# Linear attention with complex gates and an MLP on one core: another order table for all five engines, and the ACT table loads listed up front

## The chip, the cores and the metric

The kernel runs on one core of a Trainium2 chip. A core has a matrix engine (TensorE, PE in the profile), three engines for element-wise work (VectorE is DVE, ScalarE is ACT, GpSimd is POOL) and queues for transfers, of which this kernel uses the one of SyncE (SP). Each engine works through its own list of instructions in the order in which it was written, and waits at the head of its list until what that instruction needs has been made. The metric is the device time of the whole program in microseconds, the median of several runs. The profile is one more execution, recorded by the hardware profiler.

## The reference

```python
# q, k, v, a_re, a_im: (B=4, H=8, S=768, D=48)
mag = sqrt(a_re**2 + a_im**2)
scale = minimum(mag, 0.999) / (mag + 1e-6)
a = scale * (a_re + 1j * a_im)
for t in range(S):                      # S_ is D x D for each batch and head
    S_ = a[:, :, t, :, None] * S_ + k[:, :, t, :, None] * v[:, :, t, None, :]
    y[:, :, t] = einsum('bhd,bhde->bhe', q[:, :, t], S_.real)
x = y.transpose(0, 2, 1, 3).reshape(3072, 384)
h = x @ w_in                            # 384 x 2048
g = h * tanh(log1p(exp(h)))
out = g @ w_out                         # 2048 x 384
```

All tensors are fp32. In the kernel the recurrence over time becomes, for each chunk of 128 tokens, two small matrix products for each head: products of q and k inside the chunk, weighted by the running product of the gates, and a term with the state that the chunk before left.

## The kernel before, in words

The 3072 tokens are worked in 12 units of 256, three units to a batch, each of two chunks of 128. A unit passes through three stages, and while one unit is in the MLP the next ones are in the earlier stages.

The first stage, `ew_steps`, works out the running product of the gates: its size through logarithms and exponentials, its angle through an arctangent, sums along time and sines. ACT does the functions and DVE most of the rest. ACT needs one function table for logarithm and exponential and another for arctangent and sine, and a table load (`ACT_TABLE_LOAD`) stands between stretches of the two kinds. `window` holds the steps of a unit that need the second table. `phi2` (L456) is the step that brings an angle into one turn. The stage ends in `turn1` and `turn2`, which multiply q and k by the product (L497) and send the result through DMAs (`relay`, L493) into the tile `T`, in which heads instead of channels lie on the partitions.

The second stage, `attn_steps`, is made, for each chunk, of these parts: `pkn`, a transpose of k on PE (L569) that ACT copies into the tile `kn` (L570); `pa`, the products of q and k (L613, later units L601), which DVE masks into `am` (L615, L604); `ypsum`, the sum of `am` times v and of q times the old state (L628), which ACT copies to `y` (L633); `pd`, the new part of the state, from `kn` and v (L648), which DVE adds to the state `S` (L653, L655, L656); and DMAs that turn `y` into the rows `xf` of the MLP (L669, L682).

The third stage, `moe_steps`, runs over 8 pairs of 128 columns of the hidden layer: `ph` is the first product (L715; for the first half of the first unit L711, which takes plain fp32 operands), an elementwise chain `e` on ACT and DVE makes g from it (L719 to L725, on ACT recorded as L250), g is split into a coarse and a fine part (`gh`, `gl`, L282 and L283), `po` is the second product (L752, L748), and DVE evicts it as `o` (L767), which a DMA writes out (L768). Three terms (coarse times coarse, fine times coarse, coarse times fine) make a product here, so `ph` and `po` are by far the most work of PE.

The weights arrive as 64-bit integers in which the bits of the given numbers lie, one tile `raw0` to `raw15` for each block (L303). Each is converted by one ACT operation (recorded as L250), two DVE operations (L313, L314) and an addition on POOL (L316), and later split (L282, L283).

`spin` puts 84 filler matmuls (`junk`, L540) into PE's list, on a constant tile; nothing reads their result. 40 of them wait for the first `phi2`, 44 for the copy to `y`.

What sets the order of the work: the program is first written down stage by stage, and then `in_order` chains the instructions of each engine by the table `ORDER`, a text for each of PE, DVE, Activation, Pool and SP. A number is an instruction's place among those of its engine as written, and "+n" stands for n that follow each other. So the engine's list is exactly the table's:

```python
for run in text.split():
    first, _, count = run.partition("+")
    for n in range(int(first), int(first) + int(count or 1)):
        if last is not None:
            tc.add_manual_dep(own[n], last.name, order, reason="order of the engine")
        last = own[n]
```

Of the kernel before, what the change touches and what calls it, by code (L numbers as in the profile page):

```python
# [28 lines left out]
TU = 256  # L29
NU = S // TU  # L30
UNITS = B * NU
# [24 lines left out]
KU = 3  # L56
PU = 3
# [952 lines left out]
```

## Time and profile before

| | us |
|---|---|
| median of 3 runs | 573.38 (571.77 to 573.8) |
| the profiled execution's own time | 573.63 |
| its span in the trace | 571.9 |
| PE busy in the span | 547.7 (96%) |
| DVE busy | 481.1 (84%) |
| ACT busy | 469.4 (82%) |
| POOL busy | 40.5 (7%) |

The span runs from the first recorded work of the program to its last; the run's own time is 1.7 us longer. Busy shares are means over the whole span, and the stages have different limits, so the shares alone don't say what the time hangs on. Matmuls overlap each other in their pipeline, so starts are a better guide than durations when one counts what a matmul costs. A matmul of fp32 operands can show as two records. The mean granted clock of PE over the span is 0.993.

### The profile page before, as it was taken

Reading aid. Unit: us, or ns where it says so; the run is one execution under the profiler, and the core shown is the slowest. Engines: PE = TensorE matmul, PEld = TensorE weight load, DVE = VectorE, ACT = ScalarE, POOL = GpSimd, SP = SyncE. Lnnn points to the kernel's source line nnn. Section 1 sums busy time; section 2 is a strip of 40 time slices with the busy share of each in tenths; the row PEclk is TensorE's granted clock in tenths of the full one; section 3 lists DMA queues with packets and bytes.
Section 4 is the critical chain, followed back from the end, with each engine's and each line's share of the span. In section 5 each row is a group of like instructions: output and inputs, shape, how many; then the busy total and the mean of one; then the engine's idle time right before and its main releaser. Section 6 shows DMA issues by size and latency. Waiting matters only on the chain.

```text
span 571.9 us, 13326 instructions
## 1 busy us (share of the span) xinstructions
PE 547.7 (96%) x5254; PEld 509.9 (89%) x5254; DVE 481.1 (84%) x865; ACT 469.4 (82%) x753; POOL 40.5 (7%) x55
## 2 busy tenths in 40 slices
PE   0889999999999999999999999999999999999996
PEld 0458878789999999999999999999999999999996
DVE  6989999999999998988988999887897887554543
ACT  6898999999987899799898988888978777446662
POOL 2111413330010000000000000000000000000000
PEclk9979999999999999999999999999999999999999
DMA  8778935906553647606547437317426425301000
GB/s 281 241 237 261 329 118 139 278 22 193 162 164 107 188 126 191 170 16 182 142 137 202 132 91 226 115 36 216 139 75 173 116 70 145 105 21 37 1 29 32
DMA packets 69059, 80.69 MB, mean 141 GB/s; under 512 B 6144, under 2 KB 60672, under 8 KB 68992
## 3 DMA queue, kind: packets, MB, share of 16 engines
q1 hardware_dynamic: 68992, 79.80, 47.1%
q8 instruction: 42, 0.69, 0.5%
q14 instruction: 25, 0.20, 0.1%
HBM read 44.63 MB, written 11.40 MB: 98 GB/s over the span
## 4 chain that ended last, share of the span: by engine, by line
PE 93%; DVE 2%; DMA 2%; SPq 1%; ACT 0%; issue 0%; DVEq 0%
PE ph L715 35%; PE po L752 33%; PE ypsum L628 7%; PE pa L601 5%; PE po L748 4%; PE pd L648 3%; PE junk L540 2%; PE ph L711 2%; PE pa L613 2%; DMA raw<-w_in 1%; PE pkn L569 1%; SPq L350 1%; DMA T<-QK 0%; SPq L357 0%; DVE X L497 0%
## 5 line engine op out<-in xcount | busy, mean ns | idle before, releaser
L715 PE MATMUL ph<-xH,w 128*128 128x256 f32 x1104 | 226.1, 287 | 0.0
L752 PE MATMUL po<-w,gh 128*128 128x384 f32 x704 | 202.9, 339 | 0.0
L250 ACT ACTIVATE e<-e 128x512 f32<-128x512 f32 (+1 forms) x300 | 177.2, 609 | 19.8 <-DVE e L720 17.2
L715 PEld LDWEIGHTS ph<-xH,w 128*128 128x128 f32 x1104 | 180.9, 190 | 2.8 <-issue 0.8
L715 PE MATMUL ph<-xL,w 128*128 128x256 f32 x552 | 156.0, 283 | 0.0
L752 PEld LDWEIGHTS po<-w,gh 128*128 128x128 f32 x704 | 129.4, 189 | 2.1 <-issue 1.3
L752 PE MATMUL po<-w,gl 128*128 128x384 f32 x352 | 118.8, 337 | 0.0
L715 PEld LDWEIGHTS ph<-xL,w 128*128 128x128 f32 x552 | 104.8, 190 | 1.4 <-issue 0.8
L250 ACT ACTIVATE e<-ph 128x512 f32<-128x512 f32 (+1 forms) x100 | 57.1, 572 | 42.9 <-PE ph L715 34.7
L725 DVE SCALAR_TENSOR_TENSOR g<-e,ph 128x512 f32<-128x512 f32 (+1 forms) x100 | 65.7, 657 | 20.1 <-ACT e L250 16.5
L752 PEld LDWEIGHTS po<-w,gl 128*128 128x128 f32 x352 | 66.3, 188 | 0.2
L720 DVE TENSOR_SCALAR e<-e 128x512 f32<-128x512 f32 (+1 forms) x100 | 41.2, 412 | 28.3 <-ACT e L250 28.1
L283 DVE TENSOR_TENSOR gl<-g,gh 128x512 fp32r<-128x512 f32 x88 | 59.9, 682 | 2.9 <-ACT gh L282 2.5
L258 ACT ACT_TABLE_LOAD x47 | 60.3, 1283 | 1.6 <-PEq L966 0.8
L250 ACT ACTIVATE X<-X 128x768 f32<-128x768 f32 (+1 forms) x70 | 51.4, 747 | 3.0 <-DVE X L397 1.9
L540 PE MATMUL junk<-cmask 128*128 128x512 bf16 x84 | 24.2, 443 | 15.4 <-DVE I L456 15.4
L628 PE MATMUL ypsum<-am,V 128*48 128x128 f32 x240 | 36.1, 273 | 1.0 <-DVE am L615 1.0
L316 POOL TENSOR_TENSOR raw<-raw 128x768 int32<-128x768 int32 x16 | 28.5, 1782 | 93.9 <-DVE raw L314 47.2
L282 ACT CAST gh<-g 128x512 fp32r<-128x512 f32 x40 | 24.6, 614 | 10.9 <-PE po L752 10.6
L540 PEld LDWEIGHTS <-cmask 128*128 128x128 bf16 x84 | 9.1, 112 | 27.2 <-issue 21.8
L628 PE MATMUL ypsum<-T,S 96*48 96x128 f32 x320 | 32.5, 277 | 0.0
L250 ACT ACTIVATE X<-R 128x768 f32<-128x768 f32 (+1 forms) x40 | 29.6, 757 | 1.0 <-DVE R L433 1.0
(88 smaller groups left out, 757.3 us busy)
## 6 DMA issues: line engine op xcount, KB each, us to landing
T<-X SPq DMA_DIRECT2D x72, 129.0 KB, 2.5
T<-QK SPq DMA_DIRECT2D x72, 129.0 KB, 2.5
raw<-w_in SPq DMA_DIRECT2D x8, 768.0 KB, 7.1
raw<-w_out SPq DMA_DIRECT2D x8, 768.0 KB, 6.6
kd<-vx SPq DMA_DIRECT2D x45, 128.0 KB, 2.8
kn<-kd SPq DMA_DIRECT2D x15, 384.0 KB, 3.1
V<-v SPq DMA_DIRECT2D x12, 384.0 KB, 4.0
out_dram<-o SPq DMA_DIRECT2D x24, 192.0 KB, 2.2
```

The lines of the kernel that those rows point to most:

```text
L250: ins = nc.scalar.activation(out, in_, func, **kw)
L258: ins = nc.scalar.preload_act_table_set(name)
L282: heng(h, src)
L283: leng(out=lo, in0=src, in1=h.bitcast(F32), op=ALU.subtract)
L316: nc.gpsimd.tensor_tensor(hi, hi, lo, ALU.add)
L540: ins = nc.tensor.matmul(junk, cmask, cmask.unsqueeze(1).broadcast_to([P, 4, P]), start=True, stop=True)
L601: nc.tensor.matmul(pa[row:row + C // 2, i, hi * C // 2:], T[:, 1, hi * C // 2:][:, :C // 2], T[:, 0, hi * C // 2:C], start=True, stop=True)
L628: nc.tensor.matmul(py[64 * par:64 * par + D, i, :], lhs, rhs, start=n == 0, stop=first or n == 1)
L715: nc.tensor.matmul(ph[:, a, :], rows_in(parts[j][:, wp], kt, a), st[xp][:, kt, :], start=n == 0, stop=n == 8)
L720: nc.vector.tensor_scalar_min(e, e, math.exp(20.0))
L725: nc.vector.scalar_tensor_tensor(g, e, 2.5, ph, ALU.subtract, ALU.mult)
L752: nc.tensor.matmul(po[t], gp[:, a, tsl], rows_out(parts[NPAIR + j][:, wp], a), start=j in starts and a == 0 and n == 0, stop=j + 1 in ends ...
```

## The change

Three things are edited. The table `ORDER` is replaced by another for all five engines; it was reached from the old one by moving single instructions. The ACT table loads, which were written where the stretch of each kind began (by `with_trig`, with `act` and `act_set` around them), are now written ahead of everything as one list, `SETS`, and the order table puts them into ACT's list; there are 45 of them instead of 47. And `ew_steps` gets a branch for units from `PIPE` on; as `PIPE` is 99 and there are 12 units, it is never taken.

```diff
+PIPE = 99
...
 ORDER = {
     "PE": """
-        0+24 40+4 48+16 24+4 44+4 28+8 64+16 124+12 36+4 80+16 188+6 96+4 136+4 226+3 248+3 100+4 251+3 229+3 156+16
...
+        0+10 48 40 49 44+2 52+4 50+2 41+2 10+4 46+2 14 43 15+4 56+4 19+12 60+4 31+4 64+15 35+5 79 124+8 80+19 132+4
...
+SETS = "l t l t l t l t l t l t l t l t l t l t l t l t l t l t l t l t l t l t l t l t l t l t l t l t l"
...
-    def with_trig(*parts):
-        prev = act_set("trig_and_small", fence["since"] + [fence["last"]])
-        for part in parts:
-            if callable(part):
-                part()
-                continue
-            for out, in_, func, kw in part:
-                ins = nc.scalar.activation(out, in_, func, **kw)
-                after(ins, prev)
-                prev = ins
-        fence["last"] = act_set("natural_log_exp_and_others", [prev])
-        fence["since"] = []
-
-    fence["last"] = act_set("natural_log_exp_and_others", [])
+    for name in SETS.split():
+        nc.scalar.preload_act_table_set({"l": "natural_log_exp_and_others", "t": "trig_and_small"}[name])
+
+    act = nc.scalar.activation
...
+        def run(ops):
+            for out, in_, func, kw in ops:
+                act(out, in_, func, **kw)
+
         def window(gs=groups):
-            with_trig(arctan(gs), lambda: [f() for f in each(phi1, phi2, gs=gs)], sines(gs))
+            run(arctan(gs))
+            for f in each(phi1, phi2, gs=gs):
+                f()
+            run(sines(gs))
...
+        elif u < PIPE:
+            steps += each(size, slope) + [lambda: run(arctan())]
+            steps += each(test, phi1, mag1, mag2, phi2, mag3, mag4, mag5)
+            steps += [lambda: run(sines())] + each(grow)
         else:
-            steps += each(size, slope) + [lambda: with_trig(arctan())]
-            steps += each(test, phi1, mag1, mag2, phi2, mag3, mag4, mag5)
-            steps += [lambda: with_trig(sines())] + each(grow)
+            before = units[u - 1].get("sines", list)
...
-    def moe_steps(st, row0, unit=UNITS, cut=False, act=act, slot=range(UNITS * NPAIR, (UNITS + 1) * NPAIR)):
+    def moe_steps(st, row0, unit=UNITS, cut=False, slot=range(UNITS * NPAIR, (UNITS + 1) * NPAIR)):
```

In the kernel after, a line number below the table is smaller: the filler L540 is L528 there, `pkn` L569 is L557, `pa` L613 is L601, `ypsum` L628 is L616, `pd` L648 is L636, `ph` L711 is L699. What ACT records before as L250 and L270 has the line of the step itself.

Three places show what the table does. The first is PE's list at the start of the program, from the last of the first block of fillers on. Before:

```order
L540 MATMUL junk<-cmask 128x512
L569 MATMUL pkn<-ident,T 128x96 x4
L613 MATMUL pa<-T 128x128 x8
L628 MATMUL ypsum<-am,V 48x128 x8
L540 LDWEIGHTS cmask
```

The first row is the last of 24 fillers. In the changed list it is the last of ten, and behind it stands:

```order
L528 MATMUL junk<-cmask 128x512
L601 MATMUL pa<-T 128x128
L557 MATMUL pkn<-ident,T 128x96
L601 MATMUL pa<-T 128x128
L557 MATMUL pkn<-ident,T 128x96 x2
L601 MATMUL pa<-T 128x128 x6
L557 MATMUL pkn<-ident,T 128x96 x2
L528 LDWEIGHTS cmask
```

14 of the first fillers have moved behind the first products of `T`, and the first `ypsum`, which needs DVE's mask, comes later, behind further fillers.

The second place is ACT's list around the copies of k (`kn`) of the first unit's chunks; the number behind a tile's name tells its allocations apart. `pkn_455` and `pkn_461` are the second chunk's transposes before; `raw1_115`, `raw2_122` and so on are blocks of weights. Before:

```order
L633 COPY y_379<-ypsum_94 112x512
L570 COPY kn_96<-pkn_286 128x384
L250 ACTIVATE X1_251<-X1_251 128x384
L250 ACTIVATE raw2_122<-raw2_122 128x768
L250 ACTIVATE X_252<-R_153 128x3x128 x4
L570 COPY kn_96<-pkn_455 128x384
L258 ACT_TABLE_LOAD
L270 ACTIVATE I_154<-I_154 128x384 x2
L570 COPY kn_96<-pkn_461 128x384
L250 ACTIVATE raw3_126<-raw3_126 128x768
```

In the changed list the same tiles have other numbers (`pkn_499` and `pkn_493` are the second chunk's transposes):

```order
L621 COPY y_417<-ypsum_138 112x512
L411 ACTIVATE X_292<-R_197 128x3x128
L410 ACTIVATE X_292<-R_197 128x3x128
L247 ACT_TABLE_LOAD
L486 ACTIVATE I_198<-I_198 128x384 x2
L284 ACTIVATE raw8_509<-raw8_509 128x768
L372 ACTIVATE X_826,good_142<-R_505 128x6x128
L558 COPY kn_140<-pkn_499 128x384
L375 ACTIVATE X_826<-I_506 128x6x128
L284 ACTIVATE raw1_159<-raw1_159 128x768
L558 COPY kn_140<-pkn_493 128x384
```

The two copies now stand behind the table load, the arctangents, two weight conversions and two squares of the next unit (L372, L375); before, the first stood ahead of the table load and the second directly behind the arctangents.

The third place is PE's list at the first `ph` of the MLP. Before, fillers and that `ph` read:

```order
L540 MATMUL junk<-cmask 128x512
L711 MATMUL ph<-xf,raw_113 128x128 x6
L540 LDWEIGHTS cmask
L540 MATMUL junk<-cmask 128x512
L540 LDWEIGHTS cmask
```

Three more fillers, four `pa` and the next `ph` follow. In the changed list:

```order
L528 MATMUL junk<-cmask 128x512
L616 MATMUL ypsum<-am,V 48x128 x2
L616 MATMUL ypsum<-T,S 48x128
L699 MATMUL ph<-xf,raw_157 128x128 x6
L528 LDWEIGHTS cmask
L528 MATMUL junk<-cmask 128x512
L601 MATMUL pa<-T 128x128
L636 MATMUL pd<-V,kn 33x48
```

Products of the second and third chunk that stood behind the first `ph` now stand ahead of it, in part; counted from the start of PE's list to that `ph`, there were 56 fillers, 12 `pa`, 16 `pkn`, 8 `ypsum` and 16 `pd` before, and there are 63, 15, 16, 15 and 27 now.

## Rows read from the trace of the kernel before

**Rows 1.** The page's chain that ended last, by line: share of the span.
```profile
PE ph L715 35%; PE po L752 33%; PE ypsum L628 7%; PE pa L601 5%; PE po L748 4%; PE pd L648 3%; PE junk L540 2%; PE ph L711 2%; PE pa L613 2%; DMA raw<-w_in 1%; PE pkn L569 1%; SPq L350 1%; DMA T<-QK 0%; SPq L357 0%; DVE X L497 0%
```

**Rows 2.** PE's waits: us in total, how many, the longest.
```profile
PE junk L540 <- DVE I L456: 15.4, 1, 15.4
PE pkn L569 <- DMA T<-QK: 2.0, 2, 1.7
PE ypsum L628 <- DVE am L615: 1.0, 1, 1.0
PE pd L648 <- ACT kn L570: 0.8, 1, 0.8
```

**Rows 3.** Busy by stretch: length, PE, PEld, DVE, ACT, POOL (count), granted clock, DMA share, GB/s.
```profile
15.40:21.40 6.00, 5.95 (x15) 2.14 (x16) 5.86 (x11) 5.86 (x11) 0.00 (x0) 1.00 0.36 110
21.40:24.00 2.60, 2.31 (x11) 0.87 (x9) 2.60 (x7) 2.17 (x3) 0.00 (x0) 1.00 0.81 223
...
35.00:41.90 6.90, 6.37 (x24) 4.19 (x25) 5.29 (x15) 5.72 (x10) 1.78 (x1) 0.51 0.86 265
...
55.00:140.00 85.00, 85.00 (x703) 71.66 (x702) 84.27 (x140) 82.46 (x137) 24.49 (x18) 1.00 0.58 179
...
375.00:425.00 50.00, 50.00 (x532) 48.30 (x529) 43.54 (x80) 42.41 (x66) 1.15 (x2) 1.00 0.43 124
...
567.00:571.90 4.90, 0.01 (x1) 0.00 (x0) 0.56 (x1) 0.00 (x0) 0.00 (x0) 0.90 0.24 84
```

**Rows 4.** PE in order of time, to the first ph: start, us, operation, idle before.
```profile
15.45 8.27 PE L540 MATMUL junk<-cmask 128*128 128x512 bf16 x24 [15.45 <-DVE I L456]
24.08 0.52 PE L569 MATMUL pkn<-ident,T 96*128 96x96 f32 x4 [0.37 <-DMA T<-QK]
...
44.67 1.57 PE L711 MATMUL ph<-xf,raw 128*128 128x128 f32 x12
```

**Rows 5.** The chain from 44 to 66 us: start, us, piece, records.
```profile
49.41 0.86 PE junk L540 x4
...
51.68 1.00 PE pd L648 x24
52.68 1.82 PE ypsum L628 x32
54.50 0.81 PE pkn L569 x8
...
56.05 1.85 PE pa L613 x16
```

**Rows 6.** DVE in order of time, 48 to 53 us.
```profile
48.96 0.95 DVE L314 SCALAR_TENSOR_TENSOR raw<-raw,wx 128x768 uint32<-128x768 uint32 x1
...
52.79 0.55 DVE L655 TENSOR_TENSOR S<-pd,S 96x384 f32<-96x384 f32 x1 [1.41 <-PE pd L648]
```

**Rows 7.** POOL in order of time, 49 to 56 us.
```profile
50.05 2.06 POOL L316 TENSOR_TENSOR raw<-raw 128x768 int32<-128x768 int32 x1 [11.71 <-DVE raw L314]
```

**Rows 8.** The page's group of ACT's table loads: busy, mean ns, idle before.
```profile
L258 ACT ACT_TABLE_LOAD x47 | 60.3, 1283 | 1.6 <-PEq L966 0.8
```

**Rows 9.** ACT in order of time, 36 to 44 us.
```profile
36.44 0.48 ACT L570 COPY kn<-pkn 128x384 f32<-128x384 f32 x1 [0.30 <-PE pkn L569]
...
39.07 0.46 ACT L570 COPY kn<-pkn 128x384 f32<-128x384 f32 x1
...
42.35 0.83 ACT L250 ACTIVATE X<-R 128x768 f32<-128x768 f32 x1
...
43.59 0.91 ACT L250 ACTIVATE raw<-raw 128x768 int32<-128x768 uint32 x1
```

**Rows 10.** SP's queue in order of time: issue of a weight block.
```profile
33.53 0.60 SPq L303 DMA_DIRECT2D raw<-w_out  x1
```

**Rows 11.** Weight transfers: that issue, then the page's group: KB, us to landing.
```profile
raw<-w_out SPq DMA_DIRECT2D x1, 768.0 KB, 5.1
...
raw<-w_out SPq DMA_DIRECT2D x8, 768.0 KB, 6.6
```

More of the change, by code (lines that the diff above doesn't have):

```diff
@@ L75 @@
     "PE": """
[44 rows of a table removed]
[44 rows of a table added]
     """,
     "DVE": """
[29 rows of a table removed]
[29 rows of a table added]
     """,
     "Activation": """
[24 rows of a table removed]
[23 rows of a table added]
     """,
     "Pool": """
-        8 3+2 1 5 10 0 7 9 6 2 11+9 21 20 22+5 30 28+2 31 27 34 36 33 32 35 38 37 40 39 51 41+2 44 43 45+2 48 47 49+2
+        10 0+2 8 3 9 4 2 11 13 5 12 14+5 21 19+2 22+5 28 27 29 7 31 30 33 32 34 6 35+2 38 37 39+2 42 41 43+2 51 45+2
+        48 47 49+2
     """,
     "SP": """
[13 rows of a table removed]
[13 rows of a table added]
     """,
 }
+SETS = "l t l t l t l t l t l t l t l t l t l t l t l t l t l t l t l t l t l t l t l t l t l t l"
 def in_order(tc, nc):
@@ L240, in tile_kernel @@
     nc.gpsimd.memset(rmask[:, :, 0:1], 0.0)
-    NOSYNC = mybir.DependencyInfo(mybir.DependencyClass.NoSync, mybir.DependencyReason.DATA)
-    fence = {"last": None, "since": []}
-    def after(ins, prev):
-        if not ORDER:
-            tc.add_manual_dep(ins.ins, prev.ins.name, NOSYNC, reason="activation table order")
-    def act(out, in_, func, **kw):
-        ins = nc.scalar.activation(out, in_, func, **kw)
-        if func in (AF.Exp, AF.Ln):
-            if fence["last"] is not None:
-                after(ins, fence["last"])
-            fence["since"].append(ins)
-        return ins
-    def act_set(name, prevs):
-        ins = nc.scalar.preload_act_table_set(name)
-        for p in prevs:
-            after(ins, p)
-        return ins
-    def with_trig(*parts):
-        prev = act_set("trig_and_small", fence["since"] + [fence["last"]])
-        for part in parts:
-            if callable(part):
-                part()
-                continue
-            for out, in_, func, kw in part:
-                ins = nc.scalar.activation(out, in_, func, **kw)
-                after(ins, prev)
-                prev = ins
-        fence["last"] = act_set("natural_log_exp_and_others", [prev])
-        fence["since"] = []
-    fence["last"] = act_set("natural_log_exp_and_others", [])
+    for name in SETS.split():
+        nc.scalar.preload_act_table_set({"l": "natural_log_exp_and_others", "t": "trig_and_small"}[name])
+    act = nc.scalar.activation
     raw = {}
@@ L525, in ew_steps @@
             steps += [window]
-        else:
-            steps += each(size, slope) + [lambda: with_trig(arctan())]
-            steps += each(test, phi1, mag1, mag2, phi2, mag3, mag4, mag5)
-            steps += [lambda: with_trig(sines())] + each(grow)
+        elif u < PIPE:
+            steps += each(size, slope) + [lambda: run(arctan())]
+            steps += each(test, phi1, mag1, mag2, phi2, mag3, mag4, mag5)
+            steps += [lambda: run(sines())] + each(grow)
+        else:
+            before = units[u - 1].get("sines", list)
+            st["sines"], st["turns"] = sines, each(turn1, turn2)
+            steps += each(size, slope) + [lambda: run(before() + arctan())] + units[u - 1].get("turns", [])
+            steps += each(test, phi1, mag1, mag2, phi2, mag3, mag4, mag5, grow)
+            if u + 1 == UNITS:
+                steps += [lambda: run(sines())] + st["turns"]
+            return steps
         for g in groups:
@@ L956, in general @@
             split(px, st["xH"][:, :, sl], st["xL"][:, :, sl], nc.scalar.copy, nc.vector.tensor_tensor)
-        first, second = moe_steps(st, u * TU, act=nc.scalar.activation)
+        first, second = moe_steps(st, u * TU)
         for j in range(NPAIR + LAG):
```

217 rows, old and new, of the table ORDER are left out of this document.

## The prediction, made before the changed kernel was run

> **What bounds the kernel now.** I read four views, from the coarse to the fine. First the chain that ended last: it is matmuls of PE almost to the end, most of them `ph` and `po` of the MLP [rows 1]. Then PE's waits: there are four, and the last of them ends at 35.5 us [rows 2]. Third, busy time by stretch: from 55 to 140 us and from 375 to 425 PE is busy for the whole stretch, and in the first of the two DVE has 84.3 and ACT 82.5 of 85 us, so there three engines are full at once; in the second DVE and ACT have 6 to 8 us to spare [rows 3]. Fourth, PE's own order of time up to 46 us: fillers (`junk`) until 24, then attention matmuls with gaps, and the first `ph` at 44.67 [rows 4]. From there PE ran without a gap to its last matmul at 567.0, and 4.9 us of last eviction and output followed [rows 3]. So an order can change the time in three ways only: when the first `ph` starts, how much of PE's list stands behind that point, and how many new gaps come into the dense part.
>
> The rows also show a clock. The first 15 fillers took 5.95 us, 0.40 each, and the next 11 took 2.31, 0.21 each; one level is half the other, so these are 1.2 and 2.4 GHz, although the granted clock column says 1.00 for both. It fell once more: from 35.0 to 41.9 the granted clock was 0.51 [rows 3], behind gaps of up to 1.7 us [rows 2].
>
> **The change, step by step.** The instructions are the same but for two ACT table loads less; all else is order.
>
> Step 1, the start of PE. Before, 24 fillers ran from 15.45 until `T` had landed at 24.1 [rows 4]; the changed list has ten there, then `pa` and `pkn` of the same `T`. I find nothing in the lists of DVE, ACT and SP ahead of that `T` that would bring it earlier, so I leave it at 24.1. Ten fillers at 0.40 end at 19.5, and PE stands still for 4.6 us. I take it that the clock is then at its lower level when `T` comes, and that raising it costs as much as at the first start: 15 fillers with 0.19 too much each, 2.9 us, say 3.0. The bounds: nothing (the ten fillers were enough), and 6.4, if it falls again as at 35.0, where half of 6.9 us was lost, 3.4.
>
> The Trainium skill, page "TensorE: Matmul & The Clock Gate", section "Part 1: The HAM clock gate (the "warmup" mystery)", says that the slow clock is the resting state and activity lifts it. The rows agree at 21.4 and at 35.0. By that rule the 4.6 us without a matmul put PE back to the slow level, as in my sum; if the fillers' effect lasted over the gap, the sum would be 3.0 us lower.
>
> Step 2, from `T` to the first `ph`. The changed list has 53 more fillers, 15 `pa`, 16 `pkn`, 15 `ypsum` and 27 `pd` there. At full clock, from [rows 5]: a filler is 0.215 (0.86 by 4), a `pa` 0.231 (1.85 by 8), a `pkn` 0.10 (0.81 by 8), a `ypsum` 0.114 (1.82 by 16; its rows show two records for a matmul, as do those of `pa` and `pd`), a `pd` 0.0625 (1.00 for the 16 of a chunk). That is 11.4 + 3.5 + 1.6 + 1.7 + 1.7 = 19.9 us. With 3.0 for the clock and 0.4 for short waits on evictions the first `ph` starts at 24.1 + 23.3 = 47.4, 2.7 later than before. Can PE be fed so fast? I followed the producers down the lists with the durations of before: the masked `am` for the first `ypsum` at about 29.4, the second chunk's `T` at 36.0, the copies of `pkn` at 42 and 44, the first `xf` at 44.9. Each lies 0.2 to 1.7 us ahead of PE, closest the copies of `pkn` (a rival below).
>
> Step 3, what is no longer behind the first `ph`. Before, 56 of the 84 fillers, 12 `pa`, 8 `ypsum` and 16 `pd` stood ahead of it; now 63, 15, 15 and 27. So the dense part is shorter by 7 × 0.215 = 1.5, 3 × 0.231 = 0.7, 7 × 0.114 = 0.8 and 11 × 0.0625 = 0.7: 3.7 us. Step 2 and 3 together: 2.7 − 3.7 = −1.0. Put otherwise: PE does the same work, loses 3.0 to a second cold start and some 0.5 more idle at `T`, and saves the fall of the clock at 35.0 (3.4) and about a microsecond of its later gaps.
>
> Step 4, the dense part. Just behind the first `ph`, DVE waited 1.41 us for `pd` before it could update `S` [rows 6]; most of that `pd` now stands ahead of `ph`, so the wait goes, and DVE comes to the MLP's evictions about 1 us earlier, in spite of PE's later start. That matters, as DVE and ACT are full until 140 us: if they came later, PE's gain would be lost there. The fourth `ph` group needs weights that go through DVE's conversion (0.95 us, [rows 6]) and POOL's addition (2.06, [rows 7]); I get 53.0 for them, and PE comes to it at about 53.2, so no wait. The rest of the dense part is the same work in another order on five engines. Before, it had no gap at all, and a new list can hardly do better; there are some hundred places where a `ph` or `po` needs a bank that DVE or ACT has to free. I put 0.4 us on it, an estimate; below 0 nothing is to be had, and above it I allow 3 us, about twice the 1.41 us that DVE waits in [rows 6], once in the full stretch and once later.
>
> Step 5, the table loads. Two of 1.283 us [rows 8] are gone from ACT, 2.6 us. They are those between the last two units' windows of trigonometric functions, at about 380 to 425 us, where ACT was busy for 42.4 of 50 us and PE for all 50 [rows 3]. So this time is hidden: I cost it at nothing. If the cover were gone (ACT last at the front of PE), it would be worth up to 2.6.
>
> Step 6, the end. The last `po`, its eviction and the output are in the order of before, save that a small test (`okay`, one element) comes after the last eviction on DVE and not ahead of it; the last output is written meanwhile. Nothing.
>
> The sum: +2.7 − 3.7 + 0.4 = −0.6. The profiled execution took 573.63, which gives 573.0; the median of the three runs is 0.25 lower than the profiled one, so I predict 572.8.
>
> **The rivals.** A difference under 0.5%, 2.9 us, can't be told from none here; the three chances are cut at that.
>
> First rival, slower: PE waits for ACT's copies of `pkn`. Before, ACT made them directly behind the arctangents and the table load, at 36.4 and 39.1 [rows 9]. In the changed list the conversion of `raw8` (0.91, as for the other weights) and a square of 0.83 [rows 9] stand ahead of the first, and another square and the conversion of `raw1` ahead of the second. So a copy that feeds PE's `pd` now stands behind a weight transfer. Before, it was issued at 33.5 and took 5.1 us to land [rows 10, 11]; I put it 0.7 us later, landing at 39.3, which gives the copies at 42.0 and 44.0, just in time. The median of these transfers is 6.6 [rows 11]. It decides from a landing of 39.7 on; at 6.6 the copies are 1.1 us late, the fillers there can't be used as they stand in line behind the `pd`, and the clock can fall as it did at 35.0, for 3.4 more. Then first `ph` is at 48.5 to 52 and the time 574 to 577.5, with the clock's fall 577. For it speaks the queue as it stands, against it that the fillers around it are spread among the `pd`.
>
> Second rival, faster: the fillers' effect lasts, or PE reaches its full level soon after 24.1. Then the 3.0 us of step 1 are not lost; PE is bounded by `xf` at 44.9 in place of 44.4, so first `ph` starts at about 44.9, and the sum is 0.2 − 3.7 + 0.4 = −3.1: 570.3. For it: the clock column reads 1.00 until 35.0 in spite of the gaps at 24. Against it: the first fillers were slow for 6 us and there are now fewer of them. DVE and ACT would give some of it back between 55 and 140, so 571 is as likely as 570.
>
> Third rival: the change does nothing that is seen, as DVE and ACT and not PE decide from 55 to 140 us, and any shift ahead of it is absorbed: −1.0 goes to 0, new waits of 0.4 stay, 574.0, or 573.8 on the scale of the runs. It ends on the same side of the bound as the forecast.
>
> **How the numbers follow.** The forecast (steps 1 to 6, within 1.5 us of 572.8, that is 571.3 to 574.3) has 0.40, the third rival 0.15, the first 0.22, the second 0.18; 0.05 is left for a mishap in the dense part of over 3 us. Faster by over 0.5% is a time under 570.5: half of the second rival and a tenth of the forecast's spread toward it, 0.14. Slower is one over 576.3: two thirds of the first rival and the mishap, 0.2. That leaves 0.66 for the same. The range goes from 570.0 (the second rival's end) to 577.0 (the first rival's), with about 1 in 10 on either side left out.
>
> **What would show it.** Right: in the changed kernel ten fillers at 0.40 us, then a wait of PE of over 4 us for `T`; `pa` at 0.5 us each behind it; no granted clock of 0.5 later; the first `ph` between 46 and 48.5; at most 1 us of waits of PE behind it; ACT's table loads 45, with the same stretch dense on PE. Wrong: `T` at another time than 24.1, a PE wait for `kn` of more than 1 us, `pa` at 0.25 directly behind `T`, or waits of PE of more than 2 us after 55 us.

## The result, and the profile after

The changed kernel takes 579.5 us (median of 6 runs, 579.3 to 581.5), the kernel before 573.4; the ratio is 1.0122, 95% interval 1.0103 to 1.0141. It is 1.2% slower. (The ratio weighs all runs, whose means are 580.0 and 573.0; the medians differ by 6.1 us, 1.07%.) The forecast was 572.8, with a range to 577.0, so the time lies outside it. The profiled execution took 581.5, the longest of the six, so its rows hold some 2 us more than the median.

PE's waits in the changed kernel (us in total, times, longest):

```profile
PE junk L528 <- DVE I L429: 15.7, 1, 15.7
PE pa L601 <- DMA T<-QK: 4.3, 1, 4.3
PE ypsum L616 <- DVE am L603: 1.1, 2, 0.8
PE ypsum L616 <- ACT X L397: 0.9, 1, 0.9
PE ypsum L616 <- DVE S L644: 0.5, 1, 0.5
PE pd L636 <- DMA kn<-kd: 0.5, 1, 0.5
PE ph L703 <- DVE xL L256: 0.2, 1, 0.2
```

The 4.3 us ahead of `T` are those that step 1 spoke of. Those behind it come to 3.2 us, and the kernel before had none behind 35.5 us [rows 2]. But PE's busy time went up as well, from 547.7 to 551.9 us, with the same 5254 records. As I read it, a matmul that starts a little late while the one before it is still in the pipeline shows as busy, not as a wait. So I compared starts. The page of the kernel after begins:

```profile
PE 551.9 (95%) x5254; PEld 512.9 (88%) x5254; DVE 485.8 (84%) x865; ACT 470.2 (81%) x751; POOL 38.9 (7%) x55
```

PE in order of time up to the first `ph`, which answers to [rows 4]:

```profile
15.70 4.43 PE L528 MATMUL junk<-cmask 128*128 128x512 bf16 x10 [15.70 <-DVE I L429]
24.39 0.77 PE L601 MATMUL pa<-T 96*128 96x128 f32 x2 [4.27 <-DMA T<-QK]
...
25.91 2.82 PE L601 MATMUL pa<-T 96*128 96x128 f32 x12
...
49.35 1.68 PE L699 MATMUL ph<-xf,raw 128*128 128x128 f32 x12
```

Six `pa` in 2.61 us, from 25.91 to the `pkn` at 28.52, are 0.43 each, where 0.23 was the price at full speed [rows 5]: by these rows PE ran at its lower level (1.2 GHz) behind the wait, though the granted clock column reads 1.00 there. The first `ph` started at 49.35, 4.7 later than before, where I had 2.7.

How far the changed kernel is behind I read at equal work: each matmul gets the mean distance of starts that it has in the kernel before behind 60 us, fillers get nothing, and the lag is the difference of the times at which the two kernels have started the same sum.

```
time in the kernel before    50    75   100   140   200   300   566
lag of the changed kernel   2.3   3.9   4.9   6.1   5.9   7.1   8.4
```

It loses 2.3 us at the start, 3.8 more by 140 us, nothing from 140 to 200, and 2.5 behind that in this profile. By 140 us in the kernel before and 146 in the changed one all 84 fillers have run in both, so leaving them out changes nothing there. At 140 us in the kernel before and at 145.4 in the changed one PE has done the same. Busy time up to that point, first of the kernel before, then of the changed one (columns as in [rows 3]):

```profile
0.00:139.50 139.50, 120.16 (x963) 94.44 (x964) 129.87 (x233) 127.56 (x218) 34.03 (x36) 0.98 0.66 208
```

```profile
0.00:145.40 145.40, 123.30 (x963) 95.75 (x964) 133.71 (x231) 127.81 (x218) 34.04 (x38) 1.00 0.64 199
```

963 matmul records in both. DVE was busy for 129.9 and now for 133.7 us with practically the same operations, 3.8 more, and idle for 9.6 and 11.7. Busy and idle time add up to the length on every engine, so that 3.8 + 2.1 make the whole 5.9 shows nothing by itself. What marks DVE is that the same operations took longer there; on ACT they took 127.6 and 127.8. (PE's 3.1 more I read as late starts.) And of DVE's 2.1 us more of idling 1.6 lie ahead of 15 us, where no filler has run yet; the first one starts only 0.25 later for it. First the kernel before, then the changed one:

```profile
0.00:15.00 15.00, 0.00 (x0) 0.00 (x0) 9.36 (x19) 10.12 (x19) 3.86 (x15) 1.00 0.85 287
```

```profile
0.00:15.00 15.00, 0.00 (x0) 0.00 (x0) 7.78 (x19) 10.12 (x19) 3.28 (x12) 1.00 0.88 293
```

Which operations take longer? The stretches of DVE and of POOL that show it, in the changed kernel:

```profile
64.82 0.16 DVE L456 TENSOR_SCALAR_CACHE_REDUCE cnt<-QK 128x3 f32<-128x3 f32 x1
...
68.31 0.55 DVE L401 TENSOR_SCALAR X<-X 128x768 f32<-128x768 f32 x1
68.78 1.43 DVE L420 TENSOR_TENSOR I<-I,X 128x3 f32<-128x3 f32 x1
70.12 0.41 DVE L713 SCALAR_TENSOR_TENSOR g<-e,ph 128x256 f32<-128x256 f32 x1
70.45 0.68 DVE L603 TENSOR_TENSOR am<-pa,cmask 128x512 f32<-128x512 f32 x1
```

```profile
64.51 1.47 POOL L289 TENSOR_TENSOR raw<-raw 128x768 int32<-128x768 int32 x1 [2.27 <-DVE raw L287]
68.52 1.66 POOL L289 TENSOR_TENSOR raw<-raw 128x768 int32<-128x768 int32 x1 [2.54 <-DVE raw L287]
```

L420 adds three numbers for each partition and took 1.43 us; it ended at 70.21, when POOL's addition of a weight block ended (68.52 + 1.66 = 70.18). All eleven of them: 145 ns at least, 165 in the median, 1427 at most (min/median/max of that line):

```profile
L420 DVE TENSOR_TENSOR I<-I,X x11: 145/165/1427, 42.0 to 465.3; 128x3 f32<-128x3 f32 x11
```

In the kernel before the same line is L447, and none of the eleven takes long:

```profile
L447 DVE TENSOR_TENSOR I<-I,X x11: 144/159/180, 41.2 to 453.3; 128x3 f32<-128x3 f32 x11
```

There the table put something else behind POOL's start. Two places of DVE in the kernel before, with the POOL additions that ran beside them:

```profile
65.78 0.68 DVE L615 TENSOR_TENSOR am<-pa,cmask 128x512 f32<-128x512 f32 x1
66.38 0.40 DVE L725 SCALAR_TENSOR_TENSOR g<-e,ph 128x256 f32<-128x256 f32 x1
...
107.89 1.75 DVE L433 TENSOR_TENSOR_SCAN R<-rmask,R 128x768 f32<-128x768 uint8 x1
109.56 0.66 DVE L725 SCALAR_TENSOR_TENSOR g<-e,ph 128x512 f32<-128x512 f32 x1
110.14 0.68 DVE L615 TENSOR_TENSOR am<-pa,cmask 128x512 f32<-128x512 f32 x1
110.74 0.18 DVE L447 TENSOR_TENSOR I<-I,X 128x3 f32<-128x3 f32 x1
```

```profile
65.52 1.66 POOL L316 TENSOR_TENSOR raw<-raw 128x768 int32<-128x768 int32 x1 [2.94 <-DMA R<-a_re]
...
108.05 2.84 POOL L316 TENSOR_TENSOR raw<-raw 128x768 int32<-128x768 int32 x1 [3.08 <-DVE raw L314]
```

`am` and `g` read PSUM and run at their usual 0.68 and 0.40 beside POOL. POOL's own addition took 2.84 us where a DVE scan (L433, from 107.89 to 109.6, on tiles in SBUF) had begun ahead of it. So an addition of POOL and most operations of DVE that work from SBUF alone exclude each other, and the one that comes second waits until the other is through. Not all: `cnt` (L456, one small input and a sum written beside the output) took its usual 0.16 at 64.82, in the middle of POOL's addition from 64.51 to 65.98. The Trainium skill, page "SBUF — State Buffer", section "🔬 SBUF: two separate sides", has this as a rule: DVE and GpSimd share a pair of ports, held for a whole instruction, by DVE operations with two inputs there or in a fast mode, and the second one stands still. The trace agrees, with 1.28 us for an addition of three elements (1.43 less 0.15). Counted over all operations of DVE that overlap POOL and take over 0.12 us more than the low end of their form: 1.26 us behind 45 us in the kernel before, 4.17 in the changed one, 2.9 more.

### The profile page after: what moved, and what is told of

It is laid out like the page before. It is cut to its first block, busy times and chain, and to the rows that moved or that the text cites. A ratio compares the mean times of both kernels' runs of the same rounds, so it can differ in the third digit from the quotient of the medians.

```text
span 579.7 us, 13325 instructions
## 1 busy us (share of the span) xinstructions
PE 551.9 (95%) x5254; PEld 512.9 (88%) x5254; DVE 485.8 (84%) x865; ACT 470.2 (81%) x751; POOL 38.9 (7%) x55
## 4 chain that ended last, share of the span: by engine, by line
PE 69%; DVE 16%; DMA 6%; SPq 4%; issue 2%; ACT 2%; DVEq 0%; ACTq 0%
PE ph L703 27%; PE po L740 25%; PE ypsum L616 5%; PE pa L589 3%; PE po L736 3%; DMA raw<-w_in 2%; SPq L466 2%; PE pd L636 2%; PE junk L528 2%; DVE gl L256 1%; DVE g L713 1%; DMA raw<-w_out 1%; DVE X L470 1%; DMA kd<-vx 1%; PE pa L601 1%
## 5 line engine op out<-in xcount | busy, mean ns | idle before, releaser
L703 PE MATMUL ph<-xH,w 128*128 128x256 f32 x1104 | 216.0, 287 | 0.0
L740 PE MATMUL po<-w,gh 128*128 128x384 f32 x704 | 189.6, 338 | 0.0
L703 PEld LDWEIGHTS ph<-xH,w 128*128 128x128 f32 x1104 | 177.2, 191 | 3.3 <-issue 0.7
L740 PEld LDWEIGHTS po<-w,gh 128*128 128x128 f32 x704 | 127.3, 188 | 1.0 <-issue 0.2
L740 PE MATMUL po<-w,gl 128*128 128x384 f32 x352 | 117.2, 337 | 0.0
L709 ACT ACTIVATE e<-e 128x512 f32<-128x512 f32 (+1 forms) x100 | 60.9, 611 | 32.8 <-DVE e L708 32.6
L711 ACT ACTIVATE e<-e 128x512 f32<-128x512 f32 (+1 forms) x100 | 60.5, 612 | 1.9
L710 ACT ACTIVATE e<-e 128x512 f32<-128x512 f32 (+1 forms) x100 | 60.6, 611 | 1.4
L528 PE MATMUL junk<-cmask 128*128 128x512 bf16 x84 | 24.4, 425 | 15.7 <-DVE I L429 15.7
L616 PE MATMUL ypsum<-am,V 128*48 128x128 f32 x240 | 36.7, 275 | 1.1 <-DVE am L603 1.1
L616 PE MATMUL ypsum<-T,S 96*48 96x128 f32 x320 | 34.7, 277 | 1.4 <-ACT X L397 0.9
L289 POOL TENSOR_TENSOR raw<-raw 128x768 int32<-128x768 int32 x16 | 27.1, 1698 | 98.0 <-DVE raw L287 29.9
L255 ACT CAST gh<-g 128x512 fp32r<-128x512 f32 x40 | 24.4, 612 | 9.5 <-PE po L740 6.1
L528 PEld LDWEIGHTS <-cmask 128*128 128x128 bf16 x84 | 8.3, 107 | 24.6 <-issue 19.4
```

Of the source, the lines that this page charges most:

```text
L528: ins = nc.tensor.matmul(junk, cmask, cmask.unsqueeze(1).broadcast_to([P, 4, P]), start=True, stop=True)
L616: nc.tensor.matmul(py[64 * par:64 * par + D, i, :], lhs, rhs, start=n == 0, stop=first or n == 1)
L703: nc.tensor.matmul(ph[:, a, :], rows_in(parts[j][:, wp], kt, a), st[xp][:, kt, :], start=n == 0, stop=n == 8)
L709: act(e, e, AF.Square, bias=1.0)
L710: act(e, e, AF.Ln, scale=0.2, bias=0.2)
L711: act(e, e, AF.Exp, scale=-1.0)
```

## Theories, and the experiments

**Theory A**: DVE is the bound from 60 to 140 us, and 2.9 us are lost there as DVE waits for POOL. **Theory B**: the start with ten fillers is cold, DVE waits for its results, and that costs the 2.3 us of the start. **Rival C**: the order of the dense part behind 140 us has waits of its own, which cost the most. **Rival D**: neither is on the path. Ratios are to the kernel before, timed on the same chip, with 95% intervals; us are medians. A gain in us is the changed kernel's median less the run's. By the ratios the gains come out larger: 2.2 for 1.45 us (fillers), 2.9 for 1.75 (four operations), 3.2 for 2.1 (short additions), each good to about 1.8 us.

**24 fillers in front of the changed kernel.**

```diff
 "PE":
-        0+10 48 40 49 44+2 52+4 50+2 41+2 10+4 46+2 14 43 15+4 56+4 19+12 60+4 31+4 64+15 35+5 79 124+8 80+19 132+4
+        0+24 48 40 49 44+2 52+4 50+2 41+2 46+2 43 56+4 24+7 60+4 31+4 64+15 35+5 79 124+8 80+19 132+4 99+2 136+3 140+4
```

> The changed kernel, but with 24 fillers ahead of the first products of T as before (14 of the later ones moved to the front). Cold-start theory: the clock is up when T comes, the first products cost 0.25 us and not 0.5, the first ph starts 2 to 3 us earlier than 49.35 us, and the time falls by 1.5 to 3 from 579.5, to 576.5 to 578. Rival, DVE decides: the first ph comes earlier all the same, but DVE is as late as before in the stretch from 60 to 115 us, and the time falls by less than 1.

578.07 us, ratio 1.0084 (1.0059 to 1.0109). The six `pa` from 24.86 took 0.23 us each, and the first `ph` came 2.2 earlier:

```profile
24.86 1.53 PE L599 MATMUL pa<-T 96*128 96x128 f32 x12
...
47.11 1.68 PE L697 MATMUL ph<-xf,raw 128*128 128x128 f32 x12
```

The lag at 50 us went from 2.3 to 0.1, and the growth from there to 140 us stayed at 3.8: DVE kept its long operations. So the start is 1.45 us of the 6.1 in the medians, just short of the 1.5 to 3 that B expected.

**The order of before up to 50 us, then the changed one**, and **up to 140 us, then the changed one.** Each engine gets the first part of its list from one kernel and what is left in the sequence of the other; PE's table begins

```diff
 "PE":
-        0+10 48 40 49 44+2 52+4 50+2 41+2 10+4 46+2 14 43 15+4 56+4 19+12 60+4 31+4 64+15 35+5 79 124+8 80+19 132+4
+        0+24 40+4 48+16 24+4 44+4 28+8 64+16 124+12 36+4 80+16 188+6 96+4 136+4 226+3 248+3 100+4 140+4 156+11 144+3
```

in the first of the two.

> All five engines in the order of the kernel before for what that kernel had begun by 50 us, and from there in the changed order (what is left, in its sequence). Cold-start theory: the lead of 2.2 us in work that the kernel before has at 50 us is kept, so 577.3 or a little less. Theory that the loss lies between 60 and 115 us, in DVE operations that wait for POOL: no more than 2.2 gained, and the DVE operations on I still show 0.5 to 1.4 us there. If the time is 573.4, the start was everything.

> The order of the kernel before for what it had begun by 140 us, then the changed order. If the loss lies wholly ahead of 140 us (cold start and DVE behind POOL): 573.4, within 0.7. Rival, the changed order of the dense part behind 140 us has waits of its own: 575 to 576, as the lag in work of the changed kernel's profile grew from 6.1 us at 200 to 8.4 at 480.

The first took 578.33 us, 1.0091 (1.0060 to 1.0123): the start of before gives 1.2 to 1.8 back, no more, and the DVE operations that took long in the changed kernel took 0.63 to 1.62 us again. The second took 574.01, 1.0014 (0.9997 to 1.0032): nearly all of the loss lies ahead of 140 us. C is out as the main cause; 0.14% may be left for it.

**Four DVE operations moved back in the changed kernel.** The numbers are `59 89` (cnt, S), `119` (L422), `100`, `107`, `156` (L286), `121` and `177` (L420), `129` (L401), `99`, `164` (g), `96`, `181` (am), `162` (L380):

```diff
 "DVE":
-        59 89 119 100 120 105 101 129 121 99 96 107
+        59 89 100 119 120 105 101 129 99 96 107 121
...
-        145 162 156
+        145 156 162
...
-        177 181 164
+        181 164 177
```

> The changed kernel with four DVE operations moved back by one to three places each (L422 behind L286; two L420 and one L380 behind the L286 or L713 that follow), so that they don't start while POOL adds a weight block. Theory that DVE's operations on two tiles wait for POOL's addition to end: they take 0.15 to 0.95 us again in place of 0.64 to 1.63, DVE gains 2.5 to 3.5 us between 60 and 115, and the time falls to 576 to 577.5. Rival, those long operations hang on something else, or are not on the path: the time falls by less than 1.

577.76 us, 1.0072 (1.0047 to 1.0098). The three-element additions are short again:

```profile
L418 DVE TENSOR_TENSOR I<-I,X x11: 143/157/186, 41.6 to 463.0; 128x3 f32<-128x3 f32 x11
```

But L286, which now stands there, waited in their place at three of the four, for less (this is its row behind the POOL addition that began at 68.36):

```profile
69.06 0.69 DVE L601 TENSOR_TENSOR am<-pa,cmask 128x512 f32<-128x512 f32 x1
69.67 0.78 DVE L284 TENSOR_SCALAR wx<-raw 128x768 uint32<-128x768 uint32 x1
70.36 0.15 DVE L418 TENSOR_TENSOR I<-I,X 128x3 f32<-128x3 f32 x1
```

The sum of such waits behind 45 us fell from 4.17 to 1.69, 2.5 us, the growth of the lag from 50 to 140 us from 3.8 to 1.8, and the time by 1.75. A's mechanism holds; the gain is a little below its low end.

**The same, turned round: two such operations moved up in the kernel before**, one by 13 places (the row that it left is not shown), one by two.

```diff
 L656 TENSOR_TENSOR S<-S,T 96x384
+L447 TENSOR_TENSOR I<-I,X_787 128x3
 L615 TENSOR_TENSOR am<-pa,cmask 128x512
...
 L433 SCALAR_TENSOR_TENSOR R<-rmask,R 128x768
+L447 TENSOR_TENSOR I<-I,X_1036 128x3
 L725 SCALAR_TENSOR_TENSOR g<-e,ph 128x512
 L615 TENSOR_TENSOR am<-pa,cmask 128x512
-L447 TENSOR_TENSOR I<-I,X_1036 128x3
```

> The kernel before with two DVE operations of three elements for each partition (L447, 0.15 us) moved up: one by 13 places to stand ahead of two operations that read PSUM (am, g), one by two places past the same kind. Both then start while POOL adds a weight block. Theory that DVE waits for POOL's addition and that DVE is the bound from 60 to 140 us: the two take about 1.3 us each, and the time rises by 2 to 2.5, to 575.2 to 575.8. Rival, such waits are not on the path: within 0.5 of before.

575.40 us, 1.0042 (1.0025 to 1.0058). Only one of the two met POOL; the other started 0.7 us ahead of its addition and took 0.15:

```profile
108.40 1.74 DVE L433 TENSOR_TENSOR_SCAN R<-rmask,R 128x768 f32<-128x768 uint8 x1
110.07 1.36 DVE L447 TENSOR_TENSOR I<-I,X 128x3 f32<-128x3 f32 x1
```

So the row of one operation of 0.15 us, two places further up in a list of 835, grew by 1.2 us. What it is worth in the time this run doesn't settle. The 0.42% are 1.4 to 3.3 us by the interval, but the other operation had moved as well, and in the profiled execution PE waited 0.8 and 1.4 us for DMAs into `T`, ahead of both operations, where the kernel before had no such wait:

```profile
62.73 0.85 PE L569 MATMUL pkn<-ident,T 96*128 96x96 f32 x8 [1.42 <-DMA T<-X]
```

Its lag grew by 2.4 us from 50 to 75, where those waits lie, and by 1.0 from 110 to 140, where DVE waited for POOL. So about 1 us is what the collision cost in this profile. What puts D out is the changed kernel with four operations moved, whose interval (1.0047 to 1.0098) lies wholly below that of the changed kernel (from 1.0103 on).

**POOL's additions cut short**, in both kernels. Only 8 of 768 columns are added; the rest of the sum is left out.

```diff
-        nc.gpsimd.tensor_tensor(hi, hi, lo, ALU.add)
+        nc.gpsimd.tensor_tensor(hi[:, :8], hi[:, :8], lo[:, :8], ALU.add)
```

> The changed kernel with POOL's additions of the weights cut to 8 of 768 columns (the rest of the addition is left out). Theory that DVE waits behind these additions: the long DVE operations on I, wx and X are gone, DVE gains some 5 us ahead of 140 us, of which 4.2 behind 55 us, and the time falls by 3.5 to 5, to 574.5 to 576. Rival, these waits cost little: above 578.

> The kernel before with the same cut in POOL's additions. It loses only 1.2 us to such waits behind 55 us and 1.3 at 11.5 us, so the time falls by 1 to 2.5, to 571 to 572.5, and the distance to the changed kernel with the same cut is 3 to 3.5 in place of 6.1. If the distance stays at 6, the waits for POOL are no cause of the difference.

The changed kernel took 577.38 us, 1.0066 (1.0049 to 1.0084), the kernel before 573.45, 0.9994 (0.9975 to 1.0012). No DVE operation showed such a wait any more. That is worth 2.1 us in the changed kernel and nothing that can be told in the kernel before, so the distance shrinks from 6.1 to 3.9; the growth of the lag from 50 to 140 us fell from 3.8 to 1.6. The 2.1 are an upper bound for the waits, as a short addition (0.26 us in the median) also makes each block of weights ready earlier. I had expected more on both, 3.5 to 5 and 1 to 2.5. In the kernel before neither the 1.3 us of the wait at 11.5 nor the 1.26 us behind 45 came back, and in the changed one only half of the 4.17 us behind 45: with these waits gone, DVE waits more for others (in the kernel before with short additions it idled for 12.0 of the 139.6 us that the same 963 records took, where it was 9.6 of 139.5).

**Both repairs at once.** The two diffs above, together:

> The changed kernel with 24 fillers in front and with the four DVE operations moved back, both at once. If the two losses are apart from each other they add: 579.5 less 1.45 less 1.75 is 576.3. If one hides the other, about 577.7.

576.59 us, 1.0055 (1.0037 to 1.0072). They add (expected 576.3).

**Ten fillers in front of the kernel before.**

```diff
 "PE":
-        0+24 40+4 48+16 24+4 44+4 28+8 64+16 124+12 36+4 80+16 188+6 96+4 136+4 226+3 248+3 100+4 251+3 229+3 156+16
+        0+10 40+4 48+16 10+18 44+4 28+8 64+16 124+12 36+4 80+16 188+6 96+4 136+4 226+3 248+3 100+4 251+3 229+3 156+16
```

> The kernel before with 14 of its 24 first fillers moved behind the first ypsum. Cold-start theory: PE is idle for over 4 us ahead of T, the first pkn, pa and ypsum cost twice their price, am and all that hangs on it come 1 to 3 us later, DVE idles so much longer ahead of 60 us, and the time rises by 1 to 2.5. Rival, there is room enough between am and the first ph: within 0.5 of before.

573.44 us, 1.0000 (0.9985 to 1.0014): the rival. There PE had 3.5 us of waits behind the first `T` [rows 2], which took up the 14 fillers; here these waits are gone but for 0.2 us and the first `ph` even came at 43.99:

```profile
24.22 0.88 PE L569 MATMUL pkn<-ident,T 96*128 96x96 f32 x4 [4.33 <-DMA T<-QK]
...
43.99 1.57 PE L711 MATMUL ph<-xf,raw 128*128 128x128 f32 x12
```

So B holds only in part: in the order of before a cold start costs nothing. In the changed kernel it costs, and the rows show how: PE's list behind `T` is full, and DVE waits for what PE makes late. DVE's waits ahead of 60 us, first in the changed kernel, then with 24 fillers in it, where `S` is not waited for:

```profile
DVE S L641 <- PE pd L636: 1.6, 1, 1.6
...
DVE am L603 <- PE pa L601: 1.0, 1, 1.0
```

```profile
DVE am L601 <- PE pa L599: 0.3, 1, 0.3
```

**The changed order up to 55 us, then that of before**, and **up to 146 us, then that of before** (spliced as above, the other way round; PE's table begins with `0+10 48 40 49` in both).

> All engines in the changed order for what the changed kernel had begun by 55 us, and in the order of the kernel before behind it. Cold-start theory: the start's loss alone, 573.1 plus 1.2 to 2.2, 574.3 to 575.3. If the loss between 60 and 115 us comes from the later part of the table, DVE's long operations on I don't show here.

> All engines in the changed order for what the changed kernel had begun by 146 us (the point of its work that the kernel before reaches at 140), and in the order of the kernel before behind it. If the changed order loses some more behind 140 us, as the run with the first 140 us of before hinted (0.8 us over before): 578 to 579. If all is lost ahead of 140: 579.5.

The first took 579.44 us, 1.0115 (1.0093 to 1.0137), much more than the 574.3 to 575.3 expected of the start alone. DVE's long operations are gone (0.6 us in all), but DVE waits once for 2.5 us that neither kernel has there. `pa` came late, as PE had waited 2.8 us for a DMA into `T`:

```profile
67.59 0.85 PE L559 MATMUL pkn<-ident,T 96*128 96x96 f32 x8 [2.79 <-DMA T<-X]
```

```profile
71.09 0.69 DVE L605 TENSOR_TENSOR am<-pa,cmask 128x512 f32<-128x512 f32 x1 [2.49 <-PE pa L603]
```

Behind 75 us its lag doesn't grow any more. So this splice says nothing on the start; whether its order or a slow transfer made the wait, no run shows. The second took 578.89, 1.0092 (1.0068 to 1.0117), and PE has no wait behind 140 us in it, where the changed kernel had three (`S`, `kn` and `xL`, 1.2 us). The gain of 0.6 us is within the intervals.

**Three repairs at once**: 24 fillers, the four DVE operations, and the order of before behind 146 us; and **24 fillers with the short additions** (the same cut of POOL's sum as above).

> The three repairs at once: 24 fillers in front, four DVE operations moved back, and the order of the kernel before behind 146 us. If the parts add: 576.6 less about 0.8, 575.8; what is left over 573.5 is then in the first 140 us, in neither the fillers nor those four operations.

> The changed kernel with 24 fillers in front and with POOL's additions cut to 8 of 768 columns (the rest of the addition is left out). If the start and the waits for POOL are apart: 577.4 less 1.45, 575.9, and 2.4 over the kernel before are left for other causes. If the two hang together (DVE has slack left once it no longer waits for POOL): 577.

575.14 us, 1.0032 (1.0019 to 1.0046), and 575.45, 1.0031 (1.0016 to 1.0046). The parts add up in both ways, and three quarters of the 1.2% are accounted for, what lies behind 146 us (0.6 us) by its place alone. The last 0.3% is in the first 140 us, and with these runs I can't put a name to it; 1.8 us of waits for POOL and a DVE wait or two at the start are left in the first of the two kernels.

**The table loads listed up front, in the order of before.**

```diff
+SETS = "l t l t l t l t l t l t l t l t l t l t l t l t l t l t l t l t l t l t l t l t l t l t l t l"
...
-    fence["last"] = act_set("natural_log_exp_and_others", [])
+    for name in SETS.split():
+        nc.scalar.preload_act_table_set({"l": "natural_log_exp_and_others", "t": "trig_and_small"}[name])
```

> The order of the kernel before on all engines, in the changed kernel's code with its table loads listed up front, and with 45 of them (a pair with no logarithm or exponential between is dropped). If two loads less are hidden, as step 5 of the prediction says: 573.4, within 0.7. If ACT is on the path where they stood: 1 to 2.6 less.

573.72 us, 1.0003 (0.9990 to 1.0017). The list that ran has 47 entries, and its trace has the 47 loads of the kernel before, in the same order:

```profile
L247 ACT ACT_TABLE_LOAD x47 | 60.3, 1283 | 1.6 <-PEq L954 0.8
```

So, other than expected above, no load was dropped. Listing the loads up front costs nothing, and on two loads less this run says nothing. The splice with the order of before behind 146 us has 45 loads; PE has no wait behind 140 us in it, as it has none in the kernel before, so there the loads were hidden. (`SETS` of the changed kernel has 45 entries too, not the 49 that are printed with the change.)

**A try at a faster kernel**: in the kernel before, the conversion of `raw0` on ACT (number 39) moved out of the way of the first arctangents.

```diff
 "Activation":
-        0+2 3 2 4+3 9+2 39 7+2 12+2 33 11 29 15 14 16+5 34 30 32 35 22 21 23+2 36 41 48 26 25 27+2 38 37 42 40 43+2 62
+        0+2 3 2 4+3 9+2 7+2 12+2 33 11 29 15 14 16+5 34 30 32 35 22 21 23+2 36 41 39 48 26 25 27+2 38 37 42 40 43+2 62
```

> The kernel before with one ACT operation moved: the conversion of raw0, which stands ahead of the first table load of the arctangents and so ahead of T's whole chain, goes behind, next to the conversion of raw1. POOL's first addition then doesn't hold DVE's copy at 11.5 us (1.41 us for 0.15) either. If ACT's list is what T waits for, T comes 0.9 earlier and the time falls by 0.5 to 1. Rival, the time is made between 60 and 140 us by DVE, whose work is the same: within 0.4 of before.

573.14 us, 1.0000 (0.9987 to 1.0014): no gain, though `T` came at 22.9 in its profile, 1.1 earlier than in the kernel before; in the profile of the two operations moved up, whose start is that of before, it came at 23.3. Nothing that I ran beats the kernel before.

## Why the prediction was wrong

**Step 4 failed**, the dense part. I put 0.4 us on it; by the forecast's own sum it came to 5.1, as 6.1 = 4.7 − 3.7 + 5.1. I wrote that DVE "comes to the MLP's evictions about 1 us earlier, in spite of PE's later start". I had rows 3 in front of me, with DVE busy for 84.27 of 85 us, and drew from them that what DVE gains is kept, but costed only the places where PE waits for a bank. I did not go through what DVE's own operations would cost in their new places. They cost 2.9 us more, behind POOL's additions, of which the runs give back 1.75 (four operations moved) to 2.1 (all additions short). The 1.41 us wait of [rows 6] went, as I said, but `am` (1.0) and `S` (1.6) wait in its place, and a copy waits 1.3 us for POOL at 43.9. DVE came to the first `g` 1.6 us later and not 1 us earlier; first before, then now:

```profile
53.27 0.41 DVE L725 SCALAR_TENSOR_TENSOR g<-e,ph 128x256 f32<-128x256 f32 x1
```

```profile
54.83 0.42 DVE L713 SCALAR_TENSOR_TENSOR g<-e,ph 128x256 f32<-128x256 f32 x1 [0.26 <-ACT e L711]
```

Some 0.6 us more lie behind 146 us, within the intervals. The rest of the 5.1, some 2.4 us, has no cause that a run shows. The tail of up to 3 us that I allowed was for waits on banks, another thing, and still too small. The row that could have warned me was in the trace of before: a copy of DVE of six elements that took 1.41 us at 11.5 us, beside POOL's first addition:

```profile
11.51 1.41 DVE L480 COPY X<-X 128x6 f32<-128x6 f32 x1 [0.22 <-ACT X L250]
```

```profile
11.43 1.46 POOL L316 TENSOR_TENSOR raw<-raw 128x768 int32<-128x768 int32 x1 [8.22 <-DVE raw L314]
```

I took POOL, with 7% of the span, for an engine that can't matter.

**Step 1 was right as a mechanism**: ten fillers, 4.3 us of waiting, `pa` at 0.43. The granted clock did not fall again: 1.00 from 31.3 to 49.3, where the kernel before had its 0.51. (The 15 and 11 fillers that I read ahead of step 1 are 26 for 24. By their starts 14 took 0.43 each and ten 0.22, which comes to the same 2.9 us.) **Step 2 was 2 us short**: the first `ph` at 49.35 for 47.4. `T` came 0.3 later; PE stayed slow from 24.4 to about 31.3, half of 6.9 us, which is 3.4 for 3.0; the rest lies in the 18 us behind that, whose work comes to 16.2 by the prices of [rows 5], with one wait of 0.3. There, as the rows read, a change from one kind of matmul to another takes about 0.1 us beyond the price (12 fillers from 33.01 to 35.71 us: 2.70 for 2.59), and the changed list has 19 pieces in that stretch; no run tried this by itself. The copies of `pkn`, the first rival's place, were not late. **Step 3** held: what was moved ahead was moved. **Step 6** held (4.9 us of tail in both), and **step 5** as far as the splice shows it; no run tried two loads less by themselves.

**The third rival** named the right stretch, but took it that DVE and ACT would only swallow a gain. An engine that is full for 80 us can also lose time of its own, and hands on part of it: about half of 4.17 us here, by the short additions. **The second rival**'s start (24 fillers, in an experiment) gave 1.45 us (2.2 by the ratios) and not 3.0. My chance of 0.2 for slower was too small; 0.66 for the same rested on PE alone.

## What to carry to other kernels

Where an engine is full, cost a new order on that engine's own operations, with what runs beside each of them, before asking what others wait for. A busy engine's share of the span says nothing on what it blocks: POOL was busy for 7% and its additions decided about a third of the difference, most of it by operations of three elements that stood in the wrong place. Put operations that read PSUM behind the start of a POOL addition, and those on tiles in SBUF ahead of it or behind its end. And compare busy times of the same list in two runs: where the same instructions take longer, look for who shares something with them.

## What the hardware showed that I had not expected

- A DVE addition of 128x3 elements, 0.15 us by itself, takes up to 1.43 us when it starts just behind a POOL addition of 1.66; a scan of DVE that is first makes POOL's addition 2.84, where most take 1.5 to 1.7. DVE operations with an input in PSUM (`am` 0.68, `g` 0.40) run at their usual time beside POOL, and so does `cnt` (0.16).
- Ten fillers at 0.42 us each in front of a wait of 4.3 us, and with it slow first matmuls of `T`, cost the kernel before nothing (1.0000): its PE had 3.5 us of waits in that stretch, and they went.
- PE's busy time was 4.2 us longer for the same matmuls in the slower kernel, where the listed waits behind its start show 3.2 us: it can lose time that no wait in the list shows.
